# Sparse attention and a two-product ELU layer on one Trainium2 core: the second product starts three parts ahead, and the loads of batch 1 come in another order

## The chip, the core and the metric

The kernel runs on one core of one Trainium2 chip. The metric is the device time of one execution in microseconds (us). The engines of the core are PE (TensorE, with its weight loads listed apart as PEld), ACT (ScalarE), DVE (VectorE), POOL (GpSimd) and SP (SyncE). Each engine takes its instructions in program order and waits on semaphores for the others.

## The reference

Attention over 8 batches, 8 heads, 576 positions and 64 dimensions, with a local mask on the first four heads and a strided mask on the last four, and then a layer of two products with an ELU between them. The inputs are float32.

```python
def _attn_ref(q, k, v):
    scores = scale * np.matmul(q, k.transpose(0, 1, 3, 2))
    rel = pos[:, None] - pos[None, :]
    mask_local = (rel >= 0) & (rel < stride)
    mask_strided = (rel >= 0) & (pos[None, :] % stride == pos[:, None] % stride)
    ...
    return np.matmul(attn, v)

x = attn_out.transpose(0, 2, 1, 3).reshape(B * S, H * D)      # 4608 x 512
h = x @ w_in                                                  # 512 x 2048
g = np.where(h > 0.0, h, np.exp(np.minimum(h, 0.0)) - 1.0)
return g @ w_out                                              # 2048 x 512
```

## The kernel before

The attention of a batch writes its transposed result to xT (bf16, four tiles of 128 rows, 4608 columns). The 4608 tokens are cut into nine chunks of 512. For a chunk the **first product** has 16 blocks: `moe_in(nb, m)` multiplies four weight tiles of w_in with xT into one PSUM bank (four matmuls of 512 columns, line 537), ACT takes the exponential (line 559), and DVE makes block m of g from it (lines 566 and 568). In chunk 0 five of the blocks, listed in `ON_SCALAR`, take a Relu on ACT (line 562) and one DVE instruction (line 563) in place of the two.

The **second product** of a chunk has 16 parts: `moe_out(nb, i)` makes four matmuls (line 578) with g's blocks 4p to 4p+3, p = i mod 4, for the output tile i div 4. After every fourth part ACT copies the finished tile (line 582) and SP's queue writes it out. So part 3 of a chunk is the first that needs g's blocks 12 to 15.

The order on the engines is the program's order. The outer loop (line 644) runs nb from 0 to 9; in step s of 16 it issues `moe_in(nb, s)` and then `moe_out(nb - 1, s)`. So chunk nb's second product goes beside chunk nb+1's first, there is none in round 0, and the last round has the 16 parts of chunk 8 alone. The attention of batch nb+1 is cut into pieces (transposes, scores, products with v, transposes of the result) that `run(gaps, ...)` puts before and after each block. The attention of batch 0 and the first three blocks of chunk 0 are issued before the loop, in the order of the list `OPENING`.

PSUM banks are handed out by rings. `share(sc, hps, ops, ring)` (line 113) sets which banks serve the scores, the first product (hps), the second product (ops) and the rest. A ring gives the bank that was used longest ago. In round 0 hps has three banks, b_halves and singles[3], and ops has none; in rounds 1 and 2 hps has the two of b_halves and ops has singles[3]; later rounds have three banks for hps.

All loads but one go out on POOL's queue in the order of the program: batch 0, then lines 314 to 321 (w_in's first quarter, parts of batch 1 and two more quarters of w_in), then, after the code of the opening, line 631 (v of the local heads of batch 1), w_in's last quarter, w_out in four quarters and batch 2. The opening itself has no POOL instructions, so line 631 follows line 321 directly on POOL. `load_strided` issues five DMAs, `load_local` one for the early batches.

```python
for nb in range(n_chunks + 1):
    ...
    for s in range(MC):
        run(gaps, (2 * s,) if s else range(-10, 1))
        if nb < n_chunks:
            moe_in(nb, s)
        run(gaps, (2 * s + 1,))
        if nb > 0:
            moe_out(nb - 1, s)
```

Of the kernel before, what the change touches and what calls it, by code (L numbers as in the profile page):

```python
# [56 lines left out]
def kernel(  # L57
# [16 lines left out]
    MC = d_ff // 128  # L74
    N_TILE = 512
    n_chunks = n_tokens // N_TILE
# [12 lines left out]
    pair_a = ps.tile([128, 2, 512], F32, tag="pair_a")  # L89
    singles = [ps.tile([128, 512], F32, tag=f"single{i}", name=f"single{i}")  # L90
               for i in range(4)]
# [21 lines left out]
    def share(sc, hps, ops, ring):  # L113
        rings.update(sc=Ring(*sc), hps=Ring(*hps), ops=Ring(*ops), ring=Ring(*ring))
# [47 lines left out]
    def load_strided(b, name, engine=nc.gpsimd, heads=range(4)):  # L162
        rows = src[name][b, 4:8].rearrange("h (t r) d -> h t r d", r=STRIDE)
        if b == 0 and name in stage:
            t = stage[name]
        elif name == "v":
            if b not in raw:
                raw[b] = p_raw.tile([128, 4, 5, D], BF16, tag="v_raw", name="v_raw")
            t = raw[b]
        else:  # L170
            t = nat[name, "str"][b % 3].rearrange("p (h g d) -> p h g d", h=4, d=D)
        for h in heads:
            engine.dma_start(out=t[0:108, h].rearrange("p g d -> p (g d)"),  # L173
                             in_=rows[h, :, 0:30, :].rearrange(
                                 "t (r g) d -> t r (g d)", g=5))
            if h == 1:
                engine.dma_start(
                    out=t[108:126, :, 0:2, :].rearrange("p h g d -> p h (g d)"),
                    in_=rows[:, :, 30:32, :].rearrange("h t g d -> t h (g d)"))

    def load_local(b, name):
        if name == "v":

            nc.gpsimd.dma_start(
                out=v_loc[b % 3][32:128, :, :, :D].rearrange("p h i d -> p (h i) d"),
                in_=v[b, 0:4].rearrange("h (i p) d -> p (h i) d", p=LB))
            return
        flat = nat[name, "loc"][b % 3]
        if b < EARLY:
            nc.gpsimd.dma_start(  # L190
                out=flat[0:LB].rearrange("p (h x) -> p h x", h=4),
                in_=src[name][b, 0:4].rearrange("h (p j) d -> p h (j d)", j=L_RUN))
            return
        t = flat[:, 0:20 * D].rearrange("p (a i e d) -> p a i e d", a=2, i=5, d=D)
        for h in range(4):
            nc.gpsimd.dma_start(  # L196
                out=t[:, h // 2, 0:4, h % 2],
                in_=src[name][b, h, 0:512].rearrange("(i p) d -> p i d", p=128))
        for a in range(2):
            nc.gpsimd.dma_start(  # L200
                out=t[0:64, a, 4],
                in_=src[name][b, 2 * a:2 * a + 2, 512:576].rearrange("h p d -> p h d"))

    def transpose_batch(b):

        if b >= BY_DMA:
            for name, to in (("q", qT), ("k", kT)):
                nc.sync.dma_start_transpose(out=to["str"][b % 2],
                                            in_=nat[name, "str"][b % 3])
        if b >= EARLY:  # L210
            for name, to, o in (("q", qT, 0), ("k", kT, 32)):
                for a in range(2):
                    nc.sync.dma_start_transpose(
                        out=to["loc"][b % 2][:, a, o:o + 640].rearrange(
                            "p (i r) -> p i r", r=128),
                        in_=nat[name, "loc"][b % 3][:, 640 * a:640 * a + 640])

    def load_batch(b):
        for name in "qkv":
            load_strided(b, name)  # L220
        for name in "qkv":
            load_local(b, name)
# [87 lines left out]
    def load_w_in(i):  # L310
        nc.gpsimd.dma_start(out=w_in_sb[:, :, 512 * i:512 * (i + 1)],
                            in_=wi[:, :, 512 * i:512 * (i + 1)])

    load_w_in(0)
    load_strided(1, "q")
    load_strided(1, "k")
    load_w_in(1)
    load_strided(1, "v")
    load_local(1, "q")
    load_local(1, "k")  # L320
    load_w_in(2)


# [188 lines left out]
    def attention(b, start, pitch, at):  # L512


        gaps = {}
        pairs = [Pair(b, s, hp) for s in (b < EARLY, b >= EARLY) for hp in range(2)]
        if b >= EARLY:
            gaps[start] = [pairs[3].halo]
        for i, pr in enumerate(pairs):
            for off, piece in ((at[0], pr.t_q), (at[1], pr.t_k),  # L520
                               (at[7], lambda pr=pr: pr.v_in(0)),
                               (at[7] + (b > 1), lambda pr=pr: pr.v_in(1)),
                               (at[2], lambda pr=pr: pr.scores(0)),
                               (at[3], lambda pr=pr: pr.scores(1)),
                               (at[4], lambda pr=pr: pr.av(0)),
                               (at[5], lambda pr=pr: pr.av(1)),
                               (at[6] + (b > 1 and pr.strided), pr.x_out), (at[5] - 2, pr.halo if b < EARLY else lambda: None)):
                gaps.setdefault(start + pitch * i + off, []).append(piece)
        return gaps
# [42 lines left out]
    def moe_out(nb, i):  # L572
        kk, part = divmod(i, 4)
        if part == 0:
            state["ops"] = rings["ops"].next()
        ops = state["ops"]
        for m in range(4 * part, 4 * part + 4):
            nc.tensor.matmul(ops, lhsT=g_of[nb][:, m, kk * 128:(kk + 1) * 128],  # L578
                             rhs=w_out_sb[:, m, :], start=(m == 0), stop=(m == MC - 1))
        if part == 3:  # L580
            o_sb = p_o.tile([128, d_model], F32, tag="o_sb", name="o_sb")
            nc.scalar.copy(o_sb, ops)  # L582
            r0 = nb * N_TILE + kk * 128
            nc.sync.dma_start(out=out[r0:r0 + 128, :], in_=o_sb)
# [19 lines left out]
    def range_flag(row_ok16):  # L604
        cnt = rings["ring"].next()
        nc.tensor.matmul(cnt[0:1, 0:1], lhsT=row_ok16, rhs=ones, start=True, stop=True)
        nc.vector.tensor_scalar(flag, cnt[0:1, 0:1], scalar1=127.5, scalar2=None,
                                op0=ALU.is_le)

    def run(gaps, keys):  # L610
        for gap in sorted(g for g in gaps if g in keys):
            for piece in gaps[gap]:
                piece()
# [4 lines left out]
    for step in OPENING:  # L618
        pair, what = step.split(".")
        if pair == "moe":  # L620
            if step == parts[0]:
# [3 lines left out]
                b_halves = [ps_h.tile([128, 512], F32, tag=f"half{i}", name=f"half{i}")  # L625
                            for i in range(2)]
                rings["hps"] = Ring(*b_halves, singles[3])
            moe_ahead(int(what), step == parts[0], step == parts[-1])
        else:
            pairs[pair].step(what)  # L630
    load_local(1, "v")
    load_w_in(3)
    for i in range(4):
        nc.gpsimd.dma_start(out=w_out_sb[:, 4 * i:4 * (i + 1), :],
# [6 lines left out]
    opening.close()  # L641
    p_e = inner.enter_context(tc.tile_pool(name="elu", bufs=3))
    p_o = inner.enter_context(tc.tile_pool(name="o", bufs=3))
    for nb in range(n_chunks + 1):

        if nb + 1 < B:
            gaps = attention(nb + 1, *TIMES[min(nb + 1, 3)])
            if nb == 0:
                share([pair_a], b_halves + singles[3:], [], singles[:3])
            elif nb + 1 < EARLY:  # L650
                share([pair_a], b_halves, singles[3:], singles[:3])
            else:
                share([pair_a], b_halves + singles[:1], singles[3:], singles[1:3])
        else:
            gaps = {}
            share([], b_halves + singles[:1], singles[2:], singles[1:2])
        if nb + 3 < B:
            load_batch(nb + 3)
        for s in range(MC):
            if s == 6 and nb > 0 and nb + 2 < B:  # L660
                transpose_batch(nb + 2)
            run(gaps, (2 * s,) if s else range(-10, 1))
            if nb < n_chunks:
                moe_in(nb, s)
            run(gaps, (2 * s + 1,))
            if nb == B and s == 4:
                range_flag(row_ok16)
            if nb > 0:
                moe_out(nb - 1, s)
        run(gaps, range(2 * MC, 1000))  # L670
        if nb + 1 == B:
            row_ok16 = range_check()
# [163 lines left out]
```

## Time and profile before

| | |
|---|---|
| median of 3 runs | 333.73 us (332.46 to 334.82) |
| the profiled execution | 335.23 us, its span 333.4 us |
| PE busy | 309.2 us |
| DVE busy | 245.2 us |
| ACT busy | 177.0 us |
| POOL busy | 130.8 us |
| moved by DMA | 35.67 MB |

The profile is of one execution, and times in it count from the start of its span. A timeline row has the start, the duration, the engine, the line of the kernel, the operation, what it writes and reads, shapes and a count; in brackets stands the idle time of the engine before it and what ended that. A row of waits has the waiting instruction, what it waited for, the total in us, the count and the longest. Now and then a matmul's record is missing, which the counts show. A matmul's duration in a row holds its latency; how fast matmuls follow each other is read from their starts.

### The profile page before, as it was taken

Reading aid. Unit: us, or ns where it says so; the run is one execution under the profiler, and the core shown is the slowest. Engines: PE = TensorE matmul, PEld = TensorE weight load, DVE = VectorE, ACT = ScalarE, POOL = GpSimd, SP = SyncE. Lnnn points to the kernel's source line nnn. Section 1 sums busy time; section 2 is a strip of 40 time slices with the busy share of each in tenths; the row PEclk is TensorE's granted clock in tenths of the full one; section 3 lists DMA queues with packets and bytes.
Section 4 is the critical chain, followed back from the end, with each engine's and each line's share of the span. In section 5 each row is a group of like instructions: output and inputs, shape, how many; then the busy total and the mean of one; then the engine's idle time right before and its main releaser. Section 6 shows DMA issues by size and latency. Waiting matters only on the chain.

```text
span 333.4 us, 6067 instructions
## 1 busy us (share of the span) xinstructions
PE 309.2 (93%) x2198; PEld 151.9 (46%) x2238; DVE 245.2 (74%) x540; ACT 177.0 (53%) x316; POOL 130.8 (39%) x207
## 2 busy tenths in 40 slices
PE   2787888999999999999999999999999999999992
PEld 1563554455544444444444444444444444444441
DVE  6674789787888788888788878887887666866500
ACT  3644788676555655455645554556455443444220
POOL 9748736957399489329823830000000000000000
PEclk9999699999999999999999999999999999999999
DMA  6999999999999999999988995700110010001111
GB/s 111 155 116 177 177 207 117 128 119 157 165 120 131 137 200 101 125 144 180 126 136 136 143 91 121 137 31 34 49 49 33 38 59 31 31 33 42 55 66 68
DMA packets 102139, 35.67 MB, mean 107 GB/s; under 512 B 79886, under 2 KB 97494, under 8 KB 102102
## 3 DMA queue, kind: packets, MB, share of 16 engines
q0 software_dynamic: 67632, 18.10, 59.4%
q1 hardware_dynamic: 34469, 17.11, 23.8%
q8 instruction: 19, 0.31, 0.4%
q14 instruction: 19, 0.15, 0.1%
HBM read 36.70 MB, written 9.44 MB: 138 GB/s over the span
## 4 chain that ended last, share of the span: by engine, by line
PE 82%; DMA 7%; POOL 3%; DVE 2%; ACT 2%; issue 2%; POOLq 0%; ACTq 0%
PE single L578 37%; PE half L537 26%; PE single L537 9%; DMA w_in_sb<-in_moe_w_in_dram 5%; PE pair_a L425 4%; PE single L457 3%; DMA q_loc<-in_q_dram 2%; PE single L369 1%; POOL k_str L173 1%; PE single L493 1%; POOL v_raw L173 1%; DVE g_sb L568 1%; ACT e_sb L559 1%; DVE x_l L466 1%; DVE g_sb L563 0%
## 5 line engine op out<-in xcount | busy, mean ns | idle before, releaser
L578 PE MATMUL single<-w_out_sb,g_sb 128*128 128x512 bf16 x561 | 143.4, 379 | 1.1 <-issue 0.5
L537 PE MATMUL half<-xT,w_in_sb 128*128 128x512 bf16 x410 | 111.0, 388 | 2.1 <-issue 0.8
L559 ACT ACTIVATE e_sb<-half 128x512 f32<-128x512 f32 x107 | 63.9, 597 | 79.1 <-PE half L537 73.9
L566 DVE TENSOR_SCALAR e_sb<-e_sb 128x512 bf16<-128x512 f32 x139 | 63.1, 454 | 49.6 <-ACT e_sb L559 46.9
L578 PEld LDWEIGHTS <-g_sb 128*128 128x128 bf16 x576 | 52.8, 98 | 58.9 <-issue 1.1
L537 PEld LDWEIGHTS <-w_in_sb 128*128 128x128 bf16 x576 | 51.9, 100 | 55.5 <-issue 3.8
L568 DVE TENSOR_TENSOR g_sb<-e_sb,half 128x512 bf16<-128x512 bf16 x102 | 70.1, 688 | 3.8
L433 ACT ACTIVATE pr<-pair_a 128x576 bf16<-128x576 f32 (+2 forms) x60 | 39.0, 650 | 13.1 <-PE pair_a L425 13.0
L537 PE MATMUL single<-xT,w_in_sb 128*128 128x512 bf16 x141 | 39.1, 390 | 0.6 <-issue 0.2
L559 ACT ACTIVATE e_sb<-single 128x512 f32<-128x512 f32 x37 | 22.1, 598 | 26.9 <-PE single L537 23.9
L582 ACT COPY o_sb<-single 128x512 f32<-128x512 f32 x36 | 21.1, 587 | 19.1 <-PE single L578 18.4
L457 PEld LDWEIGHTS <-pr 128*128 128x128 bf16 (+3 forms) x352 | 21.8, 111 | 16.0 <-issue 3.3
L173 POOL DMA_DIRECT2D v_raw<-in_v_dram x32 | 20.2, 673 | 21.2 <-DVE v_str L408 20.8
L568 DVE TENSOR_TENSOR g_sb<-e_sb,single 128x512 bf16<-128x512 bf16 x37 | 25.5, 688 | 1.4
L173 POOL DMA_DIRECT2D k_str<-in_k_dram x32 | 20.3, 667 | 11.9 <-DMA q_loc<-in_q_dram 3.5
L173 POOL DMA_DIRECT2D q_str<-in_q_dram x28 | 17.8, 661 | 4.2 <-DMA w_out_sb<-in_moe_w_out_dram 1.7
L466 DVE TENSOR_TENSOR x_l<-single,rden 96x384 bf16<-96x384 f32 x32 | 17.7, 554 | 1.1
L466 DVE TENSOR_TENSOR x_s<-single,rden 126x256 bf16<-126x256 f32 (+1 forms) x32 | 15.7, 491 | 1.1
L440 DVE TENSOR_TENSOR pr<-pr,mask_l 128x576 bf16<-128x576 bf16 x32 | 14.4, 453 | 2.5 <-ACT pr L433 2.2
L440 DVE TENSOR_TENSOR pr<-pr,mask_s 126x504 bf16<-126x504 bf16 (+1 forms) x32 | 14.5, 453 | 1.4 <-ACT pr L433 1.4
L196 POOL DMA_DIRECT2D q_loc<-in_q_dram x16 | 12.5, 830 | 1.3 <-DMA k_str<-in_k_dram 1.0
L457 PE MATMUL single<-v_loc,pr 128*128 128x65 bf16 x192 | 12.1, 203 | 0.9 <-DVE v_loc L414 0.7
(98 smaller groups left out, 234.4 us busy)
## 6 DMA issues: line engine op xcount, KB each, us to landing
out_dram<-o_sb SPq DMA_DIRECT2D x36, 256.0 KB, 2.5
v_loc<-in_v_dram POOLq DMA_DIRECT2D x8, 288.0 KB, 9.1
k_str<-in_k_dram POOLq DMA_DIRECT2D x32, 67.5 KB, 4.7
v_raw<-in_v_dram POOLq DMA_DIRECT2D x32, 67.5 KB, 5.0
w_in_sb<-in_moe_w_in_dram POOLq DMA_DIRECT2D x4, 512.0 KB, 9.1
w_out_sb<-in_moe_w_out_dram POOLq DMA_DIRECT2D x4, 512.0 KB, 15.7
q_str<-in_q_dram POOLq DMA_DIRECT2D x28, 67.5 KB, 8.0
q_loc<-in_q_dram POOLq DMA_DIRECT2D x4, 288.0 KB, 6.8
```

Source lines behind the costliest of these rows:

```text
L173: engine.dma_start(out=t[0:108, h].rearrange("p g d -> p (g d)"), in_=rows[h, :, 0:30, :].rearrange("t (r g) d -> t r (g d)", g=5))
L425: nc.tensor.matmul(sc[:, bank, i * nq:(i + 1) * nq], lhsT=kT[kind][self.b % 2][d, at, c:c + 128], rhs=qT[kind][self.b % 2][d, at, c:c + nq ...
L433: nc.scalar.activation(halves, sc[0:nk, :, 0:w], ACT.Exp, scale=scale)
L440: nc.vector.tensor_tensor(halves, halves, m.unsqueeze(1).to_broadcast([nk, 2, w]), op=ALU.mult)
L457: nc.tensor.matmul(av[0:m, p, blk - b0, :], lhsT=self.pr[u][0:nk, o:o + m], rhs=vt[0:nk, 2 * self.hp + p, blk, :], start=True, stop=True)
L466: nc.vector.tensor_tensor(self.x[0:nq, b0:b0 + n].rearrange("q g p d -> q p g d"), av[0:nq, :, 0:n, 0:D], r.unsqueeze(3).to_broadcast([nq, ...
L537: nc.tensor.matmul(hps, lhsT=w_in_sb[:, c, m * 128:(m + 1) * 128], rhs=xT[:, c, nb * N_TILE:(nb + 1) * N_TILE], start=start, stop=stop)
L559: nc.scalar.activation(e_sb, hps, ACT.Exp)
L566: nc.vector.tensor_scalar(e1_sb, e_sb, scalar1=1.0, scalar2=1.0, op0=ALU.min, op1=ALU.subtract)
L568: nc.vector.tensor_tensor(g_of[nb][:, m, :], e1_sb, hps, op=ALU.max)
L578: nc.tensor.matmul(ops, lhsT=g_of[nb][:, m, kk * 128:(kk + 1) * 128], rhs=w_out_sb[:, m, :], start=(m == 0), stop=(m == MC - 1))
L582: nc.scalar.copy(o_sb, ops)
```

## The change

The second product runs three parts ahead. In round 0, parts 0, 1 and 2 of chunk 0 come after blocks 11, 13 and 15 of chunk 0's first product. In round nb from 1 to 8 the 16 steps hold parts 3 to 15 of chunk nb - 1 and then parts 0 to 2 of chunk nb. The last round holds parts 3 to 15 of chunk 8, 13 parts. At step 10 of round 0 the banks are shared as in round 1: hps has two, and ops gets singles[3].

The loads of batch 1 come in another order, with w_in's second quarter ahead of the strided k, the local q ahead of the strided v, and the local v ahead of w_in's third quarter. Nothing is computed otherwise than before.

```diff
     load_w_in(0)
     load_strided(1, "q")
+    load_w_in(1)
     load_strided(1, "k")
-    load_w_in(1)
+    load_local(1, "q")
     load_strided(1, "v")
-    load_local(1, "q")
     load_local(1, "k")
+    load_local(1, "v")
     load_w_in(2)
...
-    load_local(1, "v")
     load_w_in(3)
...
+    def outs(nb, s):
+        if nb == 0:
+            return [(0, i) for i in range(3) if s == 11 + 2 * i]
+        step = [(nb - 1, i) for i in range(3, MC)]
+        if nb < n_chunks:
+            step += [(nb, i) for i in range(3)]
+        return step[s:s + 1]
+
     for nb in range(n_chunks + 1):
...
         for s in range(MC):
+            if nb == 0 and s == 10:
+                share([pair_a], b_halves, singles[3:], singles[:3])
...
-            if nb > 0:
-                moe_out(nb - 1, s)
+            for chunk, i in outs(nb, s):
+                moe_out(chunk, i)
```

## The prediction

> **What bounds the kernel now.** I read the page first: its span, the busy line, and the slices of PE.
>
> ```profile
> span 333.4 us, 6067 instructions
> PE 309.2 (93%) x2198; PEld 151.9 (46%) x2238; DVE 245.2 (74%) x540; ACT 177.0 (53%) x316; POOL 130.8 (39%) x207
> PE   2787888999999999999999999999999999999992
> ```
>
> PE is below nine tenths only in the first seven of 40 slices (8.3 us each), up to about 58 us. Then I asked what PE waits for from 57.9 us to 312 us, and for the busy time of three stretches (us; PE, PEld, DVE, ACT and POOL busy; clock; DMA).
>
> ```profile
> PE single L578 <- issue: 0.5, 3, 0.2
> PE half L537 <- issue: 0.5, 3, 0.2
> PE half L537 <- DVE xT L510: 0.5, 1, 0.5
> ```
>
> ```profile
> 49.40:58.00 8.60, 7.26 (x60) 3.51 (x58) 7.64 (x18) 7.00 (x13) 5.52 (x10) 1.00 0.97 123
> 57.83:312.62 254.79, 251.93 (x1713) 119.98 (x1745) 202.15 (x426) 136.46 (x242) 91.60 (x140) 1.00 0.81 100
> 312.62:327.46 14.84, 14.73 (x66) 6.57 (x67) 1.00 0.19 73
> ```
>
> From 57.83 us, where the second product starts, to its last matmul, PE has 1.5 us of named waits and is otherwise full. So the time after 57.83 us is matmuls, and moving matmuls inside it gains nothing. In the stretch from 49.40 us, where the change puts its 12 matmuls, PE is idle for 8.60 - 7.26 = 1.34 us while DVE is busy 7.64 of 8.60. Only such holes can be filled. The first question is how much of the moved work fits there, the second what becomes late because the second product runs closer behind the first.
>
> **The price of a matmul.** A part is four matmuls of 512 columns. In the timeline (start us, us, what), the last block and the second product behind it:
>
> ```profile
> 311.76 1.03 PE L537 MATMUL half<-xT,w_in_sb 128*128 128x512 bf16 x4
> 312.62 14.84 PE L578 MATMUL single<-w_out_sb,g_sb 128*128 128x512 bf16 x66
> ```
>
> They start 0.86 us apart (312.62 - 311.76), so a part takes 0.86 us of PE and the three that move take 2.58 us. The count of matmuls stays. The last stage, now 16 parts, gets 13. So 2.58 us is the most that this move can gain.
>
> **Term 1: the three parts in chunk 0's first product.** PE, then DVE and ACT, near the end of chunk 0:
>
> ```profile
> 49.52 1.04 PE L537 MATMUL single<-xT,w_in_sb 128*128 128x512 bf16 x4
> 50.87 0.30 PE L425 MATMUL pair_a<-qT_loc,kT_loc 64*128 64x96 bf16 x6 [0.32 <-ACT pr L433]
> 51.11 1.04 PE L537 MATMUL half<-xT,w_in_sb 128*128 128x512 bf16 x4
> 52.43 1.03 PE L537 MATMUL half<-xT,w_in_sb 128*128 128x512 bf16 x4
> 56.58 0.30 PE L506 MATMUL single<-identity,x_l 96*128 96x96 bf16 x3 [0.81 <-DVE x_l L466]
> 56.72 1.27 PE L537 MATMUL half<-xT,w_in_sb 128*128 128x512 bf16 x4
> 57.83 1.02 PE L578 MATMUL single<-w_out_sb,g_sb 128*128 128x512 bf16 x4
> ```
>
> ```profile
> 52.43 0.69 DVE L568 TENSOR_TENSOR g_sb<-e_sb,single 128x512 bf16<-128x512 bf16 x1
> 56.17 0.59 ACT L562 ACTIVATE e_sb<-half 128x512 bf16<-128x512 f32 x1
> 56.92 0.64 ACT L510 COPY xT<-single 128x576 bf16<-128x576 bf16 x1 [0.16 <-PE single L506]
> ```
>
> I replay PE with the parts in. Block 11 starts at 49.52 and ends 0.86 later, at 50.38. Part 0 runs to 51.24 and covers the 0.32 us wait for the exponential. Scores (51.11 - 50.87 = 0.24) and block 12 (0.86) bring PE to 52.3, two small attention pieces to 52.8. Now the smaller ring bites: from step 10 the blocks have two banks instead of three, so block 13 needs the bank of block 11, which DVE releases at 52.43 + 0.69 = 53.12. Block 13 runs from 53.15 to 54.0: 0.3 us lost to the ring. Part 1 goes to 54.9, an attention piece to 55.05, blocks 14 and 15 to 56.8. The transposes that waited 0.81 us for x_l find it ready, because PE arrives later; they end at 57.05, and part 2 at 57.9. The next block is block 0 of chunk 1, whose last matmul needs the xT copy on ACT. ACT does block 15's exponential and Relu first, which start at 56.9 at the earliest; with about 0.5 us per step in a row (the Relu and copy above start 0.75 apart with a wait of 0.16 between) that copy ends near 58.6. So part 3 starts at about 58.85, against 57.83 for the first part before: 1.02 us later with 2.58 us of work already done. The stage yields 2.58 - 1.02 = 1.56 us. Bounds: nothing, if DVE and ACT grow by what PE fills; 2.58, if chunk 0 ends no later than now. I take the replay, because its binding times are rows.
>
> **Term 2: the last wait of the tail.** Before, 12 matmuls of parts 0 to 2 stood between the last block and part 3. After, chunk 8's part 3 comes one part behind the last block, and needs g's block 15. The weight loads there, and the last block on ACT and DVE:
>
> ```profile
> 312.41 2.04 PEld L578 LDWEIGHTS <-g_sb 128*128 128x128 bf16 x10
> 312.82 0.60 ACT L559 ACTIVATE e_sb<-half 128x512 f32<-128x512 f32 x1 [1.13 <-PE half L537]
> 313.46 0.43 DVE L566 TENSOR_SCALAR e_sb<-e_sb 128x512 bf16<-128x512 f32 x1 [0.58 <-ACT e_sb L559]
> 313.92 0.69 DVE L568 TENSOR_TENSOR g_sb<-e_sb,half 128x512 bf16<-128x512 bf16 x1
> ```
>
> Block 15 of g is done at 313.92 + 0.69 = 314.61. The first load of that part stands at 312.41 and its matmul at 312.62, 0.21 apart. Part 3 would start 0.86 later, and its fourth matmul 3 x 0.215 after that: 312.62 + 0.86 + 0.65 = 314.13, its load at 313.92. The load now waits until 314.61 and then takes about 0.1, so the matmul starts near 314.75: 0.65 us lost, which nothing hides, since only second-product matmuls are left behind it.
>
> **Term 3: the same wait at the other chunk boundaries.** There a block of the next chunk lies between, 0.86 us more. The first and the last of the seven (DVE's last write of g, then the four weight loads of the part that stands at that place now):
>
> ```profile
> 93.07 0.69 DVE L568 TENSOR_TENSOR g_sb<-e_sb,half 128x512 bf16<-128x512 bf16 x1
> 94.18 0.74 PEld L578 LDWEIGHTS <-g_sb 128*128 128x128 bf16 x4 [0.75 <-issue]
> 286.09 0.69 DVE L568 TENSOR_TENSOR g_sb<-e_sb,half 128x512 bf16<-128x512 bf16 x1
> 286.31 0.75 PEld L578 LDWEIGHTS <-g_sb 128*128 128x128 bf16 x4
> ```
>
> The fourth load starts 0.65 after the first: 94.83 and 286.96, against g at 93.76 and 286.78. Slack is 1.07 and 0.18; the five boundaries between, read the same way, give 0.18 to 0.44. Nothing waits as long as DVE keeps its times; I book 0.05 for all seven, with 0 and 5 us (the slow rival) as ends. Parts end at other steps too, so the copy of each finished output tile on ACT moves. The one bank is reused after one block of 0.86 us at the shortest, and a copy takes 0.59 us; no wait of PE for that copy appears in the list above, and I book nothing. If ACT were in the middle of a 0.6 us exponential each time, it would cost about 0.3 at each of some 24 places; the rows do not show that.
>
> **The loads.** POOL's queue issues a load when the eighth before it has landed, as counting back in its timeline shows; here k_str waits for the first quarter of w_in. The windows are one microsecond from 22 us, then the full stretch; the last number is GB/s. The last two rows are the issue of w_out and its times to landing.
>
> ```profile
> 21.65 0.60 POOL L177 DMA_DIRECT2D k_str<-in_k_dram  x1 [2.38 <-DMA w_in_sb<-in_moe_w_in_dram]
> 22.00:23.00 1.00, 0.66 (x10) 0.47 (x8) 0.95 (x4) 0.00 (x0) 1.00 (x3) 1.00 0.12 12
> 27.00:53.00 26.00, 21.66 (x212) 12.19 (x213) 18.63 (x41) 20.64 (x39) 14.60 (x22) 0.87 1.42 190
> 32.48 2.99 POOL L634 DMA_DIRECT2D w_out_sb<-in_moe_w_out_dram  x4
> DMA to landing us min/median/max: 13.0/15.7/18.6
> ```
>
> The engines stand nearly still around 22 us. With w_in's second quarter already queued there, 512 KB fill that hole, and everything later lands earlier, by 512 KB / 190 GB/s = 2.7 us as an estimate. Before, w_out lands from 32.48 + 13.0 = 45.5 on, the last about 53.3; parts 0 to 2 ask for it at 50.4, 54.0 and 57.0, so it would be in time in either order. PE has one wait that is named after a load behind 12 us:
>
> ```profile
> 35.94 1.49 PE L537 MATMUL half<-xT,w_in_sb 128*128 128x512 bf16 x3 [0.22 <-DMA w_in_sb<-in_moe_w_in_dram]
> ```
>
> It counts three matmuls of a block's four, so the gap is a record that is missing. The reorder is booked at nothing on PE. If its cover went, k_str of batch 1 would be the one to hurt: by the eighth-before rule its last piece is issued near 23.4 as now, behind data that is through by 25, and its transposes come at 29.
>
> What does reach the path is POOL's own work for batch 2, which moves into the stretch where DVE is the tight engine. DVE's L566, first where POOL works (58 to 90 us), then where it has nothing (205 to 290 us):
>
> ```profile
> L566 DVE TENSOR_SCALAR e_sb<-e_sb 128x512 bf16<-128x512 f32 x14 | 6.9, 491 | 6.3 <-ACT e_sb L559 6.0
> L566 DVE TENSOR_SCALAR e_sb<-e_sb 128x512 bf16<-128x512 f32 x45 | 19.2, 427 | 17.1 <-ACT e_sb L559 16.2
> ```
>
> Three such instructions lie between 50 and 57 us: 3 x 64 ns = 0.2 us, which I take off term 1 (1.56 becomes 1.4).
> The Trainium skill, "SBUF — State Buffer", section "Who interferes with whom", says that VectorE in a two-port mode and GpSimd exclude each other for a whole instruction. By it each of the three could wait out one POOL instruction of 0.6 us, 1.8 us in all, and the yield of term 1 would be gone; the trace has 64 ns on average, so I follow the rows.
>
> **Sum.** +1.4 - 0.65 - 0.05 = 0.7 us. The profiled execution took 335.23 us (span 333.4 and 1.8 around it) and would take 334.5. It lies 0.45% over the median of the three runs, above the highest, so I apply the difference to the median: 333.73 - 0.7 = 333.0.
>
> **The rivals.** *Nothing is filled* (0.15): DVE and ACT stretch chunk 0 by all that PE adds, for instance if POOL holds up each of the three DVE instructions for one of its own (0.60 in the k_str row). For it: DVE's 7.64 of 8.60 us. Against: the named PE waits there, 0.32 and 0.81, are PE waiting and not full. Loses term 2 alone: 334.4.
>
> *DVE late at every boundary* (0.10), the slower side. If g's block 15 comes d later, each boundary loses d minus its slack. With one more evacuation ahead (0.43 + 0.69 = 1.12): 0.05 + 2 x 0.94 + 4 x about 0.75 = 4.9 us, less the 0.7 gained: 337.9. It eats the gain from d of about 0.45 us on. Against: the order on DVE stays, and ACT's copy moves away from that place.
>
> *The half clock is not met* (0.07). One window from 32 us and one after:
>
> ```profile
> 33.00:34.00 1.00, 1.00 (x7) 0.65 (x6) 0.96 (x3) 0.40 (x1) 1.00 (x3) 0.50 1.24 191
> 39.00:40.00 1.00, 1.00 (x11) 0.33 (x10) 0.97 (x4) 0.43 (x2) 1.00 (x2) 0.97 1.50 179
> ```
>
> The clock is at 0.50 from about 32.4 to 39 us. Some 5 us of PE work in it would take 2.5 at full clock: 333.0 - 2.5 = 330.5. The three runs differ by 2.4 us, which this could be.
> The Trainium skill, "TensorE: Matmul & The Clock Gate", Part 1, has the gate judged over free-running windows of about 3.4 us, so that the phase differs by run; the dip of 6.6 us here agrees with two of them. The change touches no wait ahead of the dip, so it gets only a small chance.
>
> *All is filled and the tail does not wait* (0.06): 333.73 - 2.58 = 331.15. *The change does not do what it says* (0.04): w_out late at part 0, PE in its present place, 334 to 336.
>
> **Numbers.** The forecast has 0.58; its own range is 332.0 to 334.0. Two in ten may be left out: 330.8, which leaves out the clock case in part, to 335.6, which leaves out the upper half of the boundary case. About 1% (3.3 us) is what a measurement tells from no change. Faster by that needs 330.4, beyond the most that the move can give and so only with the clock: 0.06. Slower by that, 337.1, is the boundary case with d near one evacuation, and a little of the last: 0.09. The rest, 0.85, is within.
>
> **What would show it.** Right: the first part near 50.4 us, part 3 near 58.9, PE idle from 49.4 to 59 well under 1 us, one wait of about 0.65 us of the last chunk's part 3 for DVE's g, 52 matmuls behind the last block. Wrong: PE waits for DVE's g at each boundary, a first part that waits for w_out, a clock dip of another length, or k_str landing after 29 us.

## The result, and the profile after

The changed kernel takes 331.72 us at the median of 20 runs (330.57 to 335.02), the kernel before 333.63 us (331.77 to 337.13) in 20 runs. The ratio is 0.9943, with a 95% interval of 0.9919 to 0.9966: faster by 0.57%, 1.9 us (1.1 to 2.7), inside the stated range of 330.8 to 335.6, but below the 332.0 to 334.0 that the forecast gave for its own sum, and far more than the 0.7 us at its centre.

The page of the changed kernel's profiled execution (331.83 us), in the lines that were shown of before:

```profile
span 330.0 us, 6103 instructions
PE 308.3 (93%) x2238; PEld 150.5 (46%) x2238; DVE 246.4 (75%) x540; ACT 176.7 (54%) x316; POOL 131.5 (40%) x207
PE   1687899999999999999999999999999999999992
PEclk9999999999999999999999999999999999999998
```

The profiled executions differ by 335.23 - 331.83 = 3.4 us, more than the medians do. The last line says why, set beside that of before:

```profile
PEclk9999699999999999999999999999999999999999
```

The execution of before has a slice at 0.6, the half clock that it met behind 32 us, and the changed kernel's has none. The 3.4 us must not be read as the change's work. The granted clock was recorded for each of the 20 executions of the changed kernel: 17 have 0.994 to 0.997 and take 331.6 us on average, three have 0.984 or 0.985 and take 334.5. So a dip costs 2.85 us, and two executions can be compared only stage by stage. The medians hold dips as well. For the 20 runs of before no clock is on record, but for the 87 in the sessions of the experiments there is: 22 lie under 0.99. The 58 from 0.993 on average 333.2 us, 1.6 over the 17 of the changed kernel, so some of the 1.9 us between the medians may be a different share of dips.

PE's timeline at the end of chunk 0, one row for each of block 11, part 0, part 1, part 2, block 0 of chunk 1 and part 3:

```profile
46.94 1.04 PE L538 MATMUL half<-xT,w_in_sb 128*128 128x512 bf16 x4
47.81 1.03 PE L579 MATMUL single<-w_out_sb,g_sb 128*128 128x512 bf16 x4
...
51.45 1.03 PE L579 MATMUL single<-w_out_sb,g_sb 128*128 128x512 bf16 x4
...
54.49 1.03 PE L579 MATMUL single<-w_out_sb,g_sb 128*128 128x512 bf16 x4
55.41 1.07 PE L538 MATMUL half<-xT,w_in_sb 128*128 128x512 bf16 x4
56.32 1.02 PE L579 MATMUL single<-w_out_sb,g_sb 128*128 128x512 bf16 x4
```

The busy times of the stretch from block 11 to block 0 of chunk 1:

```profile
46.94:55.41 8.47, 8.38 (x67) 4.19 (x64) 7.29 (x17) 6.22 (x13) 5.40 (x10) 1.00 1.06 140
```

PE is idle 8.47 - 8.38 = 0.09 us here, against 1.34 us in the stretch of before. Then all waits of PE that the profile names from 57.9 us on, and the place of the second wait (PE, its weight loads, DVE):

```profile
PE half L538 <- DVE xT L511: 0.5, 1, 0.5
PE single L579 <- DVE g_sb L569: 0.4, 1, 0.4
```

```profile
311.10 1.67 PE L579 MATMUL single<-w_out_sb,g_sb 128*128 128x512 bf16 x7
313.14 1.04 PE L579 MATMUL single<-w_out_sb,g_sb 128*128 128x512 bf16 x4 [0.36 <-DVE g_sb L569]
313.13 0.33 PEld L579 LDWEIGHTS <-g_sb 128*128 128x128 bf16 x3 [0.85 <-DVE g_sb L569]
312.39 0.69 DVE L569 TENSOR_TENSOR g_sb<-e_sb,half 128x512 bf16<-128x512 bf16 x1
```

Part 2 and three matmuls of part 3 run, and the fourth waits for the last block of g, done at 313.08: the new wait at the place that was named. It is the only one for g; the seven other boundaries have none.

All kernels can be compared by stages between starts of weight loads, which repeat to about 0.02 us in the short stages when nothing holds PE up. Block n is of chunk 0 where no chunk is named; "end" is the weight load of chunk 8's last matmul.

```text
us                            block 3-5  5-8   8-11  11-chunk 1  chunk 1-chunk 8   block 15 of
                                                     block 0     block 15          chunk 8-end
before (dip)                  6.12       5.80  5.68  7.16        254.87            15.32
changed                       4.36       5.60  5.68  8.21        254.87            13.27
parts_only                    4.36       5.60  6.37  8.21        255.52            13.27
loads_only (dip)              6.37       5.52  5.67  7.17        255.22            15.32
before_fill                   4.36       5.60  6.51  7.17        254.81            15.33
after_fill                    4.35       5.60  5.67  8.21        254.83            13.27
parts_fill_dve                4.35       5.61  5.67  8.21        254.81            13.27
after_fill_dve                4.35       5.60  5.68  8.22        254.76            13.27
after_dve_tail                4.84       5.61  5.67  8.21        254.76            12.73
fill_late                     4.35       5.61  5.67  9.79        255.17            13.27
before_dve                    4.35       5.60  5.68  7.17        254.73            15.32
fill_dve_tail                 4.35       5.60  5.68  8.20        254.77            12.73
```

The work of the parts shows in two columns: chunk 0 ends 8.21 - 7.16 = 1.05 us later, the tail is 15.32 - 13.27 = 2.05 us shorter. Together 1.00 us. That leaves 0.9 us of the medians' difference to be found, less what the dips make of it.

The 4.84 us of after_dve_tail are no dip but a late load. Its clock is 1.00 there, and ACT's copy of v waits for data, and PE for the copy:

```profile
32.62 1.36 ACT L409 COPY v_str<-v_raw 126x512 bf16<-126x512 bf16 x2 [0.35 <-DMA v_raw<-in_v_dram]
33.30 0.31 PE L458 MATMUL single<-v_str,pr 126*128 126x65 bf16 x4 [1.38 <-ACT v_str L409]
```

### The profile page after: what moved, and what is told of

Its sections match the earlier page's. It is cut to its first block, busy times and chain, and to the rows that moved or that the text cites. A ratio compares the mean times of both kernels' runs of the same rounds, so it can differ in the third digit from the quotient of the medians.

```text
span 330.0 us, 6103 instructions
## 1 busy us (share of the span) xinstructions
PE 308.3 (93%) x2238; PEld 150.5 (46%) x2238; DVE 246.4 (75%) x540; ACT 176.7 (54%) x316; POOL 131.5 (40%) x207
## 4 chain that ended last, share of the span: by engine, by line
PE 86%; ACT 4%; DVE 3%; DMA 2%; issue 1%; POOL 1%; ACTq 0%; POOLq 0%; DVEq 0%
PE single L579 38%; PE half L538 29%; PE single L538 9%; PE pair_a L426 4%; PE single L458 3%; DMA q_loc<-in_q_dram 2%; PE single L370 1%; ACT pr L434 1%; ACT e_sb L560 1%; PE single L494 1%; POOL k_str L173 1%; PE single L507 1%; DVE g_sb L569 1%; DVE pr L441 0%; PE single L356 0%
## 5 line engine op out<-in xcount | busy, mean ns | idle before, releaser
L579 PE MATMUL single<-w_out_sb,g_sb 128*128 128x512 bf16 x576 | 146.2, 379 | 0.4 <-DVE g_sb L569 0.4
L538 PE MATMUL half<-xT,w_in_sb 128*128 128x512 bf16 x436 | 113.6, 382 | 0.6 <-DVE xT L511 0.5
L560 ACT ACTIVATE e_sb<-half 128x512 f32<-128x512 f32 x109 | 65.2, 598 | 80.1 <-PE half L538 75.9
L567 DVE TENSOR_SCALAR e_sb<-e_sb 128x512 bf16<-128x512 f32 x139 | 64.0, 460 | 48.1 <-ACT e_sb L560 44.5
L569 DVE TENSOR_TENSOR g_sb<-e_sb,half 128x512 bf16<-128x512 bf16 x104 | 71.5, 688 | 3.6
L538 PE MATMUL single<-xT,w_in_sb 128*128 128x512 bf16 x140 | 37.0, 383 | 0.0
L560 ACT ACTIVATE e_sb<-single 128x512 f32<-128x512 f32 x35 | 20.9, 598 | 26.4 <-PE single L538 24.4
L569 DVE TENSOR_TENSOR g_sb<-e_sb,single 128x512 bf16<-128x512 bf16 x35 | 24.1, 688 | 1.2
L173 POOL DMA_DIRECT2D q_str<-in_q_dram x28 | 18.6, 701 | 5.4 <-DMA w_in_sb<-in_moe_w_in_dram 1.8
```

The costliest lines, as they stand in the source:

```text
L538: nc.tensor.matmul(hps, lhsT=w_in_sb[:, c, m * 128:(m + 1) * 128], rhs=xT[:, c, nb * N_TILE:(nb + 1) * N_TILE], start=start, stop=stop)
L560: nc.scalar.activation(e_sb, hps, ACT.Exp)
L567: nc.vector.tensor_scalar(e1_sb, e_sb, scalar1=1.0, scalar2=1.0, op0=ALU.min, op1=ALU.subtract)
L569: nc.vector.tensor_tensor(g_of[nb][:, m, :], e1_sb, hps, op=ALU.max)
```

## Experiments

**One half of the change each.** parts_only has the parts ahead and the loads as before, loads_only the reverse.

```diff
 parts_only, against the changed kernel
-    load_w_in(1)
     load_strided(1, "k")
-    load_local(1, "q")
+    load_w_in(1)
     load_strided(1, "v")
+    load_local(1, "q")
     load_local(1, "k")
-    load_local(1, "v")
     load_w_in(2)
...
+    load_local(1, "v")
     load_w_in(3)
```

> The parts run ahead as in the changed kernel, with the loads in the order of before. Theory A (the gain is PE's holes in chunk 0 filled, about 1.5 us, less the wait in the tail, about 0.45): about 1.05 us under the kernel before among runs of the same granted clock, ratio about 0.997, and about the time of the changed kernel; w_out lands near 45.5, 48 and 50.6 us, ahead of the parts. Theory B (the order of the loads brings the gain): no faster than before, ratio 1.000 or above, since the tail wait is left alone. Theory C (the parts need the new order): the first part waits for w_out, some 2 us lost.

> The loads in the order of the changed kernel, the parts where they were before. Theory A: the same time as before among runs of the same clock, ratio 1.000 within 0.003, although w_out lands about 2.5 us earlier. Theory B: the whole gain or most of it, ratio about 0.995. A third possibility (D): the times agree within a granted clock, but fewer executions have the dip to half clock behind 32 us, so the median falls by 1 to 2 us.

parts_only: median 333.9 us of 12 runs, ratio 0.9994 (0.9961 to 1.0028). loads_only: 332.84 us, 0.9976 (0.9940 to 1.0012). Neither half alone is resolved from before. loads_only shows no fewer dips, three of 12 clocks under 0.99 against seven of 35 of before, so nothing speaks for theory D. parts_only has six of 12, and its median holds them. From 0.993 on its six executions average 333.0 us and the 25 of before 333.4: 0.4 us, not resolved either, in place of the 1.05 that theory A expected. Its stages say where the gain went: it has the 1.00 us of the parts, 13.27 in the tail and 8.21 in chunk 0, but against the changed kernel blocks 8 to 11 take 6.37 us in place of 5.68, and 0.65 us more go later. No load is late (w_out's first quarter lands 13.8 us after its issue at 33.1, at 46.9, and part 0 comes behind block 11 at 47.6). What is behind it, in parts_only: a wait of PE between 36 and 48 us, then POOL and DVE.

```profile
PE single L493 <- DVE x_s L466: 0.8, 1, 0.8
```

```profile
36.88 1.16 POOL L233 MEMSET k_str<- 32x1280 bf16 x1
37.99 1.16 POOL L233 MEMSET q_str<- 32x1280 bf16 x1
37.99 1.44 DVE L566 TENSOR_SCALAR e_sb<-e_sb 128x512 bf16<-128x512 f32 x1
39.47 0.69 DVE L568 TENSOR_TENSOR g_sb<-e_sb,single 128x512 bf16<-128x512 bf16 x1
61.80 2.35 DVE L566 TENSOR_SCALAR e_sb<-e_sb 128x512 bf16<-128x512 f32 x1 [1.09 <-ACT e_sb L559]
62.09 0.52 POOL L238 MEMSET q_loc<- 32x256 bf16 x1
...
63.35 0.52 POOL L238 MEMSET k_loc<- 32x256 bf16 x1
64.93 1.02 PE L537 MATMUL half<-xT,w_in_sb 128*128 128x512 bf16 x4 [0.64 <-DVE g_sb L568]
```

A tensor_scalar that takes 0.43 us alone takes 1.44 while POOL clears q_str, and ends 0.28 after the memset does; everything that DVE owes PE then is a microsecond late. Another takes 2.35 beside six short memsets in a row, and a block of chunk 1 waits 0.64 us for DVE behind it: these are the 0.65 us that go later. In the changed kernel the two long memsets come earlier, because the loads ahead of them on POOL's queue do:

```profile
34.53 1.16 POOL L233 MEMSET k_str<- 32x1280 bf16 x1
35.64 1.16 POOL L233 MEMSET q_str<- 32x1280 bf16 x1
```

```profile
33.44 0.89 DVE L567 TENSOR_SCALAR e_sb<-e_sb 128x512 bf16<-128x512 f32 x1
34.37 0.69 DVE L569 TENSOR_TENSOR g_sb<-e_sb,half 128x512 bf16<-128x512 bf16 x1
34.97 0.18 DVE L466 RECIPROCAL rden<-single 126x4 f32<-126x4 f32 x1
35.18 0.42 DVE L467 TENSOR_TENSOR x_s<-single,rden 126x256 bf16<-126x256 f32 x1
36.41 0.69 DVE L564 SCALAR_TENSOR_TENSOR g_sb<-e_sb 128x512 bf16<-128x512 f32 x1 [0.80 <-ACT e_sb L563]
```

Beside them DVE has other kinds of instruction, at their usual durations, and a wait of its own; no tensor_scalar falls there (the one of 0.89 us ends before them). The order alone does not ensure this. In loads_only, with the same order and a dip, one falls beside the first of them:

```profile
34.53 1.49 DVE L567 TENSOR_SCALAR e_sb<-e_sb 128x512 bf16<-128x512 f32 x1
34.58 1.16 POOL L233 MEMSET k_str<- 32x1280 bf16 x1
```

In the execution of before that was profiled, the memsets stood where the half clock had left DVE idle, so the block could not be seen:

```profile
36.20 1.16 POOL L233 MEMSET k_str<- 32x1280 bf16 x1
37.31 1.16 POOL L233 MEMSET q_str<- 32x1280 bf16 x1
38.58 0.69 DVE L563 SCALAR_TENSOR_TENSOR g_sb<-e_sb 128x512 bf16<-128x512 f32 x1 [2.33 <-ACT e_sb L562]
```

**PE kept busy through its waits.** Ten matmuls whose results nobody reads, in the kernel before and in the changed one, to take the dip out of the comparison.

```diff
         for s in range(MC):
+            if nb == 0 and s in (2, 3, 4):
+                filler("sc" if s == 2 else "ring", 4 if s == 2 else 3)
...
+    def filler(kind, n):
...
+        for _ in range(n):
+            nc.tensor.matmul(to, lhsT=w_in_sb[:, 0, 0:128], rhs=xT[:, 2, 0:N_TILE],
+                             start=True, stop=True)
```

> The kernel before with ten matmuls more whose results nobody reads, in PE's waits of about 1.1, 0.7 and 0.7 us at steps 2, 3 and 4 of round 0 (4, 3 and 3 of 512 columns, 0.86 and 0.65 us at full clock). Theory A with the clock told apart: these keep the gate open, so every execution has a granted clock near 0.995 and takes about 332.4 us, the lower of the two groups in the runs of before; the spread over executions falls from some 5 us to under 2. Rival: the dip has nothing to do with the idle time; clocks of 0.985 still come in a third to a half of the executions and the time rises by up to 0.5 us.

> The changed kernel with the same ten matmuls. Theory A: no dip, about 331.3 us in every execution, 1.0 to 1.1 us under the kernel before with the same filling: this difference is the change without the clock. Theory D (the change acts through the clock): the two filled kernels take the same time within 0.4 us.

before_fill: 332.89 us (332.03 to 334.93), ratio 0.9987 (0.9956 to 1.0017). after_fill: 331.63 us (330.57 to 333.18), 0.9933 (0.9901 to 0.9966). The filling does its work where it was put, as the stretch from 28 to 32 us shows in parts_only and then in before_fill:

```profile
28.00:32.00 4.00, 2.21 (x26) 1.35 (x25) 2.57 (x6) 3.90 (x7) 1.72 (x2) 1.00 1.35 186
```

```profile
28.00:32.00 4.00, 3.78 (x37) 1.84 (x34) 2.96 (x6) 3.69 (x8) 3.10 (x5) 1.00 1.27 167
```

Both profiled executions have no dip, and the clocks say that this is the filling's doing. Of the 64 executions of the six kernels with the filling, those below included, none has a clock under 0.99. Of the 155 of the kernels without it 40 have. Yet before_fill's spread did not fall under 2 us: four of its 12 runs lie at 334.0 and above, at clocks of 0.990 to 0.996, and why is open. The filling serves the comparison: between its two kernels the medians differ by 1.26 us, above the 1.0 to 1.1 expected (the stages of the two profiles by 1.84), and the profile of before_fill, the only one without a dip that has parts, loads and memsets where before had them, has 6.51 us between blocks 8 and 11, with a tensor_scalar of 1.22 us at 37.6. Theory D, in which the change acts through the clock, would have had them equal.

**The memsets off POOL.** This gave theory E: the order of the loads matters through where POOL's memsets fall. Batch 2's buffers are cleared on DVE behind the opening, with either order of the loads, and in the kernel before.

```diff
+    clear_v(2)
+    clear_nat(2)
+    for i in range(3):
+        clear_loc(i, nc.vector)
     load_w_in(3)
...
-    clear_v(2, nc.gpsimd)
-    clear_nat(2, nc.gpsimd)
     load_batch(2)
-    for i in range(3):
-        clear_loc(i, nc.gpsimd)
```

> The parts ahead, the loads in the order of before, the ten filling matmuls, and the clearing of batch 2's buffers (11 memsets) moved from POOL's queue to DVE, behind the opening. Theory E (the new order of the loads helps because it moves POOL's two long memsets away from a moment at which a tensor_scalar of DVE waits for them, 0.7 to 0.85 us of PE's time between blocks 8 and 11): without memsets on POOL the order of the loads no longer matters, so this takes 331.2 us, as the next kernel within 0.3, blocks 8 to 11 take 5.7 us and no tensor_scalar takes over 1 us. Rival D (the order acts through w_out, the loads themselves or the clock): still 0.7 to 2 us slower than the next kernel, blocks 8 to 11 still 6.4 us.

> The changed kernel with the filling matmuls and the same memsets on DVE. Theory E: within 0.3 us of parts_fill_dve and 0 to 0.4 us under the changed kernel with the filling (331.6), since its long memsets were already out of the way and only the six short ones near 59 us, which hold one tensor_scalar for 1.5 us, go. Rival D: 0.7 to 2 us under parts_fill_dve.

> The kernel before with batch 2's buffers cleared on DVE behind the opening, nothing else. Theory E: executions without the dip lose the 0.7 to 0.85 us between blocks 8 and 11 (5.7 us there), so the median falls by 0.4 to 0.9 us, to about 332.8; this is all that the new order of the loads brought by itself. Rival: the order of the loads brought something else; the median stays within 0.3 us of before.

parts_fill_dve: 331.86 us, ratio 0.9934 (0.9898 to 0.9970). after_fill_dve: 331.82 us, 0.9940 (0.9911 to 0.9970). With no memset on POOL the old order of the loads is as good as the new, 5.67 us against 5.68 between blocks 8 and 11, and the instruction that took 1.44 us is back, here in parts_fill_dve:

```profile
38.29 0.42 DVE L566 TENSOR_SCALAR e_sb<-e_sb 128x512 bf16<-128x512 f32 x1
```

So theory E holds for these blocks. Both medians lie 0.6 us over the 331.2 expected; the short memsets' going, expected to bring up to 0.4 us, brought nothing that the runs resolve. before_dve takes 333.03 us against 333.97 in its own session, ratio 0.9986 (0.9958 to 1.0014): the direction expected and not resolved by the times, with 5.68 us between blocks 8 and 11 in its profile. From a clock of 0.993 on its eight executions average 332.7 us and the 11 of before 333.2, which is not resolved either.

**Holes or an early start.** All three parts behind block 15, in place of one behind each of blocks 11, 13 and 15, in the changed kernel with the filling.

```diff
-            return [(0, i) for i in range(3) if s == 11 + 2 * i]
+            return [(0, i) for i in range(3) if s == MC - 1]
```

> The changed kernel with the filling matmuls, and parts 0, 1 and 2 of chunk 0 all behind block 15 and its attention pieces in place of behind blocks 11, 13 and 15. Theory A (what counts is holes filled, not an early start): the three parts no longer cover the waits of 0.3 and 0.8 us, so of the 2.59 us at most 0.3 is gained and the tail wait is paid: about 332.6 us, 1.0 to 1.3 us over the changed kernel with the filling, first block of chunk 1 about 1.2 us later. Rival (an early start counts): the same time as the changed kernel with the filling.

332.99 us, ratio 0.9975 (0.9939 to 1.0011), 1.36 us over after_fill of another session and 1.17 over after_fill_dve of its own, about as expected. Block 11 to chunk 1's first block takes 9.79 us, 1.58 more than in after_fill, where 1.2 was expected, and 2.63 more than in before: 2.59 us of matmuls moved (15.32 - 12.73, the tail without its wait) and nothing gained. PE's rows:

```profile
50.53 1.02 PE L538 MATMUL half<-xT,w_in_sb 128*128 128x512 bf16 x4 [0.57 <-DVE g_sb L569]
...
54.28 2.75 PE L579 MATMUL single<-w_out_sb,g_sb 128*128 128x512 bf16 x12
56.87 1.03 PE L538 MATMUL half<-xT,w_in_sb 128*128 128x512 bf16 x4
```

The parts stand in one piece behind the waits, and the smaller ring now shows as a wait of 0.57 us for block 11's bank, which part 0 had covered for the most part. The gain is holes filled, not an early start.

**The tail.** In the last round part 4 of chunk 8 goes ahead of part 3, into its own bank.

```diff
-            state["ops"] = rings["ops"].next()
-        ops = state["ops"]
+            state[kk] = rings["ops"].next()
+        ops = state[kk]
...
+        else:
+            step[:2] = step[1::-1]
```

> The changed kernel without the filling, with the memsets on DVE and, in the last round, part 4 of chunk 8 ahead of part 3, each of the two output tiles in its own bank. Theory A: the 0.86 us of part 4 cover the 0.52 us that part 3 waits for g's last block, so from the last block to the last matmul 12.75 us in place of 13.27, and the time falls to about 331.0 us in executions without the dip. Rival: g's last block is not what PE waits for there and the stretch stays at 13.27.

> All of it together: parts ahead, new order of the loads, filling matmuls, memsets on DVE, part 4 of chunk 8 ahead of part 3. Theory A: about 331.0 us at the median as without the filling, but no executions at 333.4 to 334.3 as there were 3 of 12 without it: from 330.2 to about 332.2. Rival: the filling does not hold the gate open, and a quarter of the executions still lies 2.5 us above the rest.

after_dve_tail: 330.9 us, ratio 0.9928 (0.9893 to 0.9964), three of 12 runs at 333.4 to 334.3, with clocks of 0.984 to 0.986. Its tail takes 12.73 us, 0.54 less, in one row without a gap:

```profile
310.74 3.62 PE L579 MATMUL single<-w_out_sb,g_sb 128*128 128x512 bf16 x16
```

fill_dve_tail: 331.04 us in six runs (329.93 to 331.79), ratio 0.9916 (0.9885 to 0.9948), the lowest ratio of all and no run of the upper kind; its six clocks are 0.996 to 1.0. Both versions beat the kernel before clearly. Against the changed kernel the 0.54 us are shown by the stage and not by the intervals, which overlap.

## Why the prediction was right, and where it was short

- **The bound.** That PE's time behind the opening is matmuls held: 254.87 us from chunk 1 to the last block in both profiles. (PE is not quite as full as the prediction says: its row has 254.79 - 251.93 = 2.86 us without PE busy, of which 1.5 are named waits.)
- **Term 1** was booked at 1.56 less 0.2. Part 0 starts 0.87 us behind block 11 and part 3 9.38 us behind it (46.94, 47.81, 56.32); the replay had 0.86 and 9.33. Chunk 0 ends 1.05 us later with 2.59 done: 1.54 us. The replay was right and the 0.2 taken off for POOL was not there: the three tensor_scalars took 0.42, 0.42 and 0.43 us.
- **Term 2**, the tail's wait, was booked at 0.65. It is 13.27 - 12.73 = 0.54 us. The mechanism was right.
- **Term 3**, the other boundaries, was booked at 0.05 and is nothing: the second and the last of the seven have 0.18 us of slack, as before. So the slow rival, DVE late at every boundary, did not come.
- **The loads** were "booked at nothing on PE", and this is the step that failed. In the changed kernel's profile no wait of PE's behind 13 us is put down to a load, as booked, though after_dve_tail, with the same order, lost 0.48 us to one (4.84 - 4.36). But the reorder also moves everything behind the loads on POOL's queue, and there stand two memsets of 1.16 us. In executions without the dip they held a tensor_scalar of DVE, which cost PE 0.69 us (6.37 - 5.68) to 0.83 (6.51 - 5.68). That adds to the parts' 1.00 us to make 1.7 to 1.8 us, inside the interval of 1.1 to 2.7. It is an account by stages of executions without the dip, and the medians hold dips, so that it comes close to the 1.9 us between them may be luck; the loads' share alone was not resolved by the times of loads_only or before_dve.
- **The range.** The parts brought 1.00 us where the sum had 0.7. The time still fell within the stated range because that had been drawn wide for the clock and for the boundaries, not because the memsets had been seen.
- **The rule not followed.** The prediction weighed what the Trainium skill, "SBUF — State Buffer", section "Who interferes with whom", says of VectorE and GpSimd against a mean of 64 ns, and took the mean. At the place in question the mean was the better guide, as the 0.42 to 0.43 us show. Beside the memsets the rule was: 0.43 us alone against 1.44 beside a memset of 1.16. The mean was over rows in which POOL mostly issues DMAs, which hold DVE little on average, and the rows of the memsets themselves were not looked at one by one.
- **The clock.** The rival that the half clock is not met gave 330.5 from 2.5 us for the dip. The dip costs 2.85 us. But the prediction took the dip of its one profile for a part of the kernel, and it comes and goes by execution in both: 22 of 87 clocks of before under 0.99 in the later sessions, three of the changed kernel's 20. Whether the change alters how often it comes is not settled by so few, nor by different sessions.

## What to carry to other kernels

When a product that fills an engine is started earlier, only the idle time that it falls into is gained: place its pieces one by one in front of the waits, and look at the other end, where less cover stands in front of the last dependence. A reordered queue moves all that stands behind it, the small instructions too, so list those and what they stand beside. And before a row of a profile is called normal, ask whether that execution was: here a clock dip hid the very conflict that the new order of the loads avoided.

## What was not expected of the hardware

A memset on POOL holds a tensor_scalar of DVE for nearly its whole length (1.44 us beside one of 1.16), and a run of six short ones, started 0.25 us apart, holds it through the run (2.35 us in parts_only). In before_fill the same run holds a copy of DVE's, 1.95 us in place of 0.35. Over the same stretches tensor_tensor and scalar_tensor_tensor keep their durations (0.42 and 0.69 us). In the profiles made without memsets on POOL no tensor_scalar behind 33 us and ahead of 62 exceeds 0.63 us, though POOL issues as many DMAs as before. Later one takes 1.01 us beside a DMA issue of 1.54 (parts_fill_dve, at 106.9 us), so issues are not always harmless.

Ten matmuls in PE's waits between 29 and 34 us, where PE had been busy 2.21 us of the 4.00 from 28 us on (parts_only), kept the half clock away: no clock under 0.99 in 64 executions, against 40 in 155 without them.
